# Decode attention with an MLP: the loop turn becomes one whole pair, and the last two V tiles come in key halves

## The chip, the cores and the metric

The kernel runs on one core of a Trainium2 chip. The metric is the device time of one execution in microseconds (us), from the first to the last instruction of the core with what lies around it; lower is better. The kernel before takes 1295.81 us, the median of three runs between 1295.5 and 1296.08.

## The reference, cut to what matters

```python
def reference(A_x, A_k_cache, A_v_cache, A_wq, A_wo, B_x, B_w1, B_b1, B_w2, B_b2):
    # B 8, one query position, D 640, 32 heads, 4096 keys, head size 128, F 1728, all bfloat16
    xn = _layernorm(A_x, axis=-1)
    q = heads(xn @ wq)                                        # [8, 32, 1, 128]
    scores = einsum("bhqd,bhkd->bhqk", q, k_cache) * 128 ** -0.5
    o = einsum("bhqk,bhkd->bhqd", softmax(scores), v_cache)
    attention = merge(o) @ wo
    h = gelu(layernorm(xn) @ w1 + b1)
    return A_x + attention + (h @ w2 + b2)
```

Each batch element and head has 4096 keys and as many values of 128 numbers. The K cache and the V cache together are 537 MB, and each number is used once.

## The kernel before, in words

**Tiles.** The work is cut into `NG` = 32 groups `g` of one batch element and eight heads. A group has a K tile and a V tile of 8 MB each. A tile is laid out as 128 partitions, 16 for each of the eight heads, by `NJ` = 256 keys by 128 numbers. K comes in two halves of 128 keys (`NKEY`), each 4 MB with a buffer of its own, so half `i` = 2g+s (s is 0 or 1) goes to `K_sb[:, s]`. V has one buffer, `V_sb`, of 8 MB for the whole tile. The code calls one group with both its K halves a pair.

**Scores of a K half.** The 128 keys are shared out. For the first 64 (`JD`), DVE multiplies K with the query, which is spread over the partitions in `qbc_sb`, adds the two halves of the products and reduces them, in three steps (`dve_chunk`). For the other 64 (`JP`), PE transposes K in eight blocks of eight keys (`pe_T`), ACT copies each block out of PSUM (`act_T`), and PE multiplies it with the queries of all eight heads (`pe_QK`). `dve_S` then selects the right head out of the eight in PSUM by a mask, and reduces; it is the select that the change moves.

**Select and PV of a group.** `dve_max` forms the maximum per head, `act_E` the exponentials `E_sb` and their row sums, and `dve_ex` spreads each weight over eight columns, all zero but that of its own head (`P_sb`, 128 x 2048). `pe_RS` adds the row sums over partitions, `dve_rinv` takes the reciprocal. `pe_PV` multiplies each of the 256 V blocks with its eight columns of P into one PSUM bank. `act_O` copies the result out, and `o_norm` scales it and stores it under a mask in `oM_sb`, on POOL for all groups but the last, on DVE for that one. Before the end `pe_ox` and `cp_ox` bring `oM_sb` into the form `oX_sb` that the product with wo needs (the first seven batch elements ahead, the eighth after the last group), `fin_wo` multiplies with wo in four pieces of 16, 10, 4 and 2 rows, and `fin_b` to `fin_d` transpose and store the output.

**Order.** All of it is written as a list of steps with a position (`at(pos, fn, ...)`, L634 to L713). Half `i` has the positions from 100 i on; sorted by position, the list gives the order of instructions on each engine. An engine runs its instructions strictly in that order and stops at a wait. All large loads are issued by SP, one after the other, into one DMA queue: in each group K half 2g+2, K half 2g+3, then V tile g+1. K half `i` waits until PE and DVE are through with half i-2 of the same buffer (`kt`, `km`), and V tile g waits until PV of group g-1 is done (`pv`). The V tile of group 30 comes in two halves, the second issued when the first has landed; that of group 31 comes whole. PV waits for the whole tile in all cases. wo's pieces are issued last.

**Prologue.** Ahead of group 0 stand the loads of wq, w1, w2 and K halves 0 and 1, the layer norms, the queries and the MLP. w1 lies in the buffer of K half 1, and w2 in that of V. So K half 1 waits for the MLP's first product and V tile 0 for its second (`mlp`) and for `pv` of the group before.

**Loop.** PE, DVE and ACT run `LOOPN` = 32 turns of a loop whose body is one group's steps; SP and POOL have straight code. `LOOP0` = -0.1 puts the border of a turn at position 200 g - 10: a turn is the select and PV of group g-1 and then the scores of group g. The first turn therefore has a select and a PV of a made-up group -1, on zeros that POOL writes to `Sd_sb` and to the part of `V_sb` that w2 does not fill (`vz`, `vz2`). The last select and PV stand behind the loop. In the sources `_replay_loop` and `looped` make the turns alike; a wait's value grows by the same step in each turn.

Of the kernel before, what the change touches and what calls it, by code (L numbers as in the profile page):

```python
# [13 lines left out]
P = 128  # L14
# [132 lines left out]
def bass_parallel_sum__gqa_block_cached__mixer_channel_mlp__decode_kernel(  # L147
# [22 lines left out]
    NQ = 2 * NG  # L170
    DC = D // P
# [5 lines left out]
    LOOP0, LOOPN = -0.1, NG  # L177
# [15 lines left out]
    with ExitStack() as es:  # L193
# [26 lines left out]
        oN_sb = sb("oN_sb", [P, HS], F32)  # L220
        head_i = sb("head_i", [P, HS], I32)
# [7 lines left out]
        oX_sb = sb("oX_sb", [P, NR, B], BF)  # L229
# [39 lines left out]
        ld_v, ld_vh = _Dma(sem("ld_v")), _Dma(sem("ld_vh"))  # L269
        ld_x, ld_b1, ld_b2, ld_wq, ld_w1, ld_w2b, st_a = (  # L270
            _Dma(sem(n)) for n in ("ld_x", "ld_b1", "ld_b2", "ld_wq", "ld_w1", "ld_w2b", "st_a"))
# [24 lines left out]
        def load_v(g, half=None):  # L296
            if half != 1:
                sp.wait(tk[("pv", g - 1)], tk["mlp"])
            else:
                sp.wait(tk[("vh", g)])  # L300
            lo, hi = (0, NJ) if half is None else (half * NKEY, (half + 1) * NKEY)
            d = ld_vh if half == 0 else ld_v
            tk[("vh" if half == 0 else "v", g)] = d.sig(sp.dma_start(
                V_sb[:, lo:hi, :], cache_src(A_v_cache, g, lo, hi)))

        def load_mlp():
            tk["w1"] = ld_w1.sig(sp.dma_start(w1_sb, B_w1.rearrange("(p c) f -> p c f", c=DC)))
            tk[("v", -1)] = tk["w2a"] = ld_v.sig(sp.dma_start(
                w2_sb[:, 0:FB, :], B_w2[0:FB * P, :].rearrange("(p c) n -> p c n", c=FB)))
            sp.wait(tk["vz"])  # L310
# [8 lines left out]
        def consts_pool():  # L319
            tk["iota"] = pool.sig(pool.iota(iota_i[:, :], [[1, P]], base=0, channel_multiplier=-1))  # L320
            tk["vz"] = pool.sig(pool.memset(M_sb[:, FB * D:(FB + 1) * D], 0.0))
            pool.memset(Sd_sb[:, :], 0.0)
# [162 lines left out]
        def dve_max(g):  # L485
            dve.wait(tk.get(("s", 2 * g + 1)), tk.get(("yr", (2 * g + 2) * NCH - 1)), tk["consts"])
# [17 lines left out]
        def dve_ex(g):  # L504
            dve.wait(tk[("E", g)], tk.get(("pv", g - 1)), tk.get(("rs", g - 1)), tk["mask8"])
            tk[("r8", g)] = dve.sig(dve.tensor_scalar(rs8_sb[:, :], mask8f[:, :], rs1_sb[:, 0:1], None, ALU.mult))
            tk[("ex", g)] = dve.sig(dve.tensor_tensor(
                P_sb[:, :, :], E_sb[:, :][:, :, None].to_broadcast([P, NJ, HS]),
                mask8b[:, :][:, None, :].to_broadcast([P, NJ, HS]), ALU.mult))
# [24 lines left out]
        def o_norm(g):  # L534
# [8 lines left out]
            if e is dve:  # L543
                PVB[0].used(dve, t)
# [267 lines left out]
```

## Time and profile before

| what | value |
|---|---|
| median of three runs | 1295.81 us |
| the profiled execution's own time | 1295.58 us |
| its span, first to last instruction | 1293.8 us |
| busy: PE, DVE, ACT, POOL | 779.9, 977.3, 581.4, 97.6 us |
| read from HBM | 551.80 MB, 427 GB/s over the span |
| V issued in the loop, issue to landing | 29.4 us, median |

The span lies 1.8 us below the execution's own time; that rest is around the instructions. In the lines of the profile below, PE is a matmul, PEld its weight load, SPq the issue of a DMA on SP's queue. A row of the timeline has the start in us, the length in us, the engine, the line, the operation, what it writes and reads with the shape, and how often; in brackets stands how long the engine was idle before it, and what ended that. Every row has line 104 because one helper records all instructions, so rows are told apart by their tiles. A row of DMA issues ends with the time from issue to landing.

### The profile page before, as it was taken

What the parts mean: (1) busy time and instruction counts of PE and PEld (TensorE: products, weight loads), DVE (VectorE), ACT (ScalarE), POOL (GpSimd) and SP (SyncE); (2) the same over time, 40 slices, a digit from 0 to 9 for tenths busy, and PEclk for the clock granted to TensorE, in tenths of its full rate; (3) what the DMA queues carried; (4) which work ended last, traced back from release to release, by engine and by line L of the source; (5) the groups of instructions that cost most, each with busy time, mean ns of one, the idle gap of its engine ahead of it and who ended that gap; (6) DMA issues with size and microseconds to landing.
All of it is one profiled execution on the core that took longest, in us unless ns stands there. A gap on an engine that the chain in (4) does not pass through costs nothing.

```text
span 1293.8 us, 38899 instructions
## 1 busy us (share of the span) xinstructions
PE 779.9 (60%) x17243; PEld 684.2 (53%) x17243; DVE 977.3 (76%) x1000; ACT 581.4 (45%) x682; POOL 97.6 (8%) x111
## 2 busy tenths in 40 slices
PE   4766655765555765654675555775555675555655
PEld 4655544654444665544564544665555565444544
DVE  4678779777779777779777779777779777779755
ACT  1544445553345553445553345554345553435532
POOL 3001000000000000000000000000000000000000
PEclk9956677776676675577766677666666775677766
DMA  9999999999999999999999999999999999999996
GB/s 395 423 421 430 431 435 432 444 426 440 418 437 433 441 426 448 412 435 434 440 428 444 419 431 435 438 428 446 420 429 436 436 436 438 422 433 431 435 428 261
DMA packets 15140, 552.01 MB, mean 427 GB/s; under 512 B 1740, under 2 KB 1813, under 8 KB 2070
## 3 DMA queue, kind: packets, MB, share of 16 engines
q1 hardware_dynamic: 15106, 551.80, 99.0%
q8 instruction: 10, 0.16, 0.1%
q14 instruction: 4, 0.03, 0.0%
q10 hardware_dynamic: 20, 0.02, 0.0%
HBM read 551.80 MB, written 0.01 MB: 427 GB/s over the span
## 4 chain that ended last, share of the span: by engine, by line
DMA 63%; PE 14%; DVE 9%; ACT 8%; issue 6%; DVEq 0%; ACTq 0%; POOL 0%; SPq 0%
DMA K_sb<-in_A_k_cache_dram 58%; ACT KT_sb L104 7%; DVE Y_sb L104 7%; PE TR_ps L104 6%; PE PV_ps L104 4%; DMA V_sb<-in_A_v_cache_dram 3%; PE S_ps L104 3%; DMA W_sb<-in_A_wq_dram 1%; DVE P_sb L104 1%; PE CH_ps L104 1%; DVE SM_sb L104 1%; DVE Sd_sb L104 0%; PE ACC_ps L104 0%; DVE mx_sb L104 0%; ACT E_sb L104 0%
## 5 line engine op out<-in xcount | busy, mean ns | idle before, releaser
L104 ACT ACTIVATE KT_sb<-TR_ps 128x1024 bf16<-128x1024 bf16 x512 | 501.4, 1022 | 100.4 <-PE TR_ps L104 97.8
L104 DVE TENSOR_TENSOR Y_sb<-K_sb,qbc_sb 128x2688 bf16<-128x2688 bf16 (+1 forms) x192 | 300.6, 1566 | 217.5 <-DMA K_sb<-in_A_k_cache_dram 217.5
L104 PE MATMUL TR_ps<-ident_bf,K_sb 128*128 128x128 bf16 x4096 | 383.9, 255 | 11.0 <-DMA K_sb<-in_A_k_cache_dram 9.8
L104 PEld LDWEIGHTS TR_ps<-ident_bf,K_sb 128*128 128x128 bf16 x4096 | 301.1, 115 | 14.3 <-DMA K_sb<-in_A_k_cache_dram 12.1
L104 DVE TENSOR_REDUCE Sd_sb<-Y_sb 128x21 f32<-128x1344 bf16 (+1 forms) x192 | 302.5, 1576 | 6.6
L104 PE MATMUL PV_ps<-P_sb,V_sb 128*128 128x8 bf16 x8448 | 230.9, 168 | 63.9 <-DVE P_sb L104 51.3
L104 PEld LDWEIGHTS PV_ps<-P_sb,V_sb 128*128 128x128 bf16 x8448 | 228.0, 104 | 67.0 <-issue 56.2
L104 PE MATMUL S_ps<-qrep_sb,KT_sb 128*128 128x8 bf16 x4096 | 193.8, 177 | 110.6 <-ACT KT_sb L104 98.2
L104 PEld LDWEIGHTS S_ps<-qrep_sb,KT_sb 128*128 128x128 bf16 x4096 | 147.3, 100 | 190.4 <-ACT KT_sb L104 187.2
L104 PE MATMUL CH_ps<-rs_sb,ones_f 128*128 128x8 f32 x66 | 19.5, 369 | 289.0 <-DVE rs_sb L104 288.8
L104 DVE TENSOR_TENSOR Y_sb<-Y_sb 128x1344 bf16<-128x1344 bf16 (+1 forms) x192 | 167.5, 873 | 6.6
L104 PEld LDWEIGHTS CH_ps<-rs_sb,ones_f 128*128 128x128 f32 x66 | 16.5, 311 | 293.6 <-ACT E_sb L104 285.9
L104 ACT ACTIVATE oU_sb<-PV_ps 128x8 f32<-128x8 f32 x32 | 5.7, 177 | 318.2 <-PE PV_ps L104 318.2
L104 POOL TENSOR_TENSOR oN_sb<-oU_sb,ri_sb 128x8 f32<-128x8 f32 x32 | 45.4, 1419 | 860.5 <-DVE ri_sb L104 806.4
L104 DVE TENSOR_TENSOR P_sb<-E_sb,mask8b 128x2048 bf16<-128x2048 bf16 x33 | 75.4, 2284 | 0.0
L104 ACT ACTIVATE qbc_sb<-CH_ps 128x128 bf16<-128x128 f32 x33 | 9.1, 277 | 134.4 <-DVE Y_sb L104 129.2
L104 ACT ACTIVATE E_sb<-Sd_sb,NB_sb 128x256 bf16<-128x256 f32 x33 | 16.7, 507 | 117.3 <-DVE NB_sb L104 117.3
L104 DVE TENSOR_TENSOR SM_sb<-S_ps,mask8f 128x512 f32<-128x512 f32 x64 | 43.6, 681 | 22.5 <-PE S_ps L104 22.5
L104 ACT ACT_TABLE_LOAD x34 | 43.6, 1283 | 8.5 <-DVE qT_sb L104 4.2
L104 DVE TENSOR_REDUCE Sd_sb<-SM_sb 128x64 f32<-128x512 f32 x64 | 43.9, 687 | 2.2
L104 POOL COPY qrep_sb<-qT_sb 128x128 bf16<-128x128 bf16 x33 | 12.8, 388 | 306.3 <-PE S_ps L104 300.9
L104 DVE TENSOR_SCALAR rs_sb<-mask8f,rs_sb 128x8 f32<-128x8 f32 x33 | 7.6, 231 | 30.0 <-ACT E_sb L104 30.0
(71 smaller groups left out, 162.7 us busy)
## 6 DMA issues: line engine op xcount, KB each, us to landing
K_sb<-in_A_k_cache_dram SPq DMA_DIRECT2D x64, 4096.0 KB, 25.5
V_sb<-in_A_v_cache_dram SPq DMA_DIRECT2D x2, 4096.0 KB, 19.5
W_sb<-in_A_wq_dram SPq DMA_DIRECT2D x1, 5120.0 KB, 15.4
W_sb<-in_A_wo_dram SPq DMA_DIRECT2D x1, 2560.0 KB, 28.0
K_sb<-in_B_w_dram SPq DMA_DIRECT2D x1, 2160.0 KB, 20.0
V_sb<-in_B_w_dram SPq DMA_DIRECT2D x1, 2080.0 KB, 25.6
W_sb<-in_A_wo_dram SPq DMA_DIRECT2D x1, 1600.0 KB, 31.3
W_sb<-in_A_wo_dram SPq DMA_DIRECT2D x1, 640.0 KB, 32.4
```

Source lines behind the costliest of these rows:

```text
L104: inst = getattr(e, name)(*a, **k)
```

## The change

- **Turn.** `LOOP0` is 0.057, so that the border of a turn is at position 200 g + 5.7: a turn is the scores of group g, its select and its PV. The made-up group, its zeros and the waits on them go; the steps run over `range(NG)`. `act_O` now also runs for group 31. V tile 0 waits for the MLP alone.
- **V.** The tiles of groups 30 and 31 (`g >= G2`) come in two key halves, each half's landing counted by a semaphore of its own (`ld_v[0]`, `ld_v[1]`), with no wait for the landing of the other. The second half of tile 30 stands in SP's queue behind K half 62, that of tile 31 directly behind its first half. PV waits for the first half ahead of matmul 0 and for the second ahead of matmul 128. For groups below 30 the whole tile counts on `ld_v[0]`; a memset of POOL at the start raises `ld_v[1]` by 16 x 30, so that the second wait has passed for these.
- **P.** `dve_ex` makes P in two products of 128 keys, and PV waits for each half.
- **Select.** `dve_S` of a group's first half goes from position 86 to 160: behind the first two of the second half's three steps on DVE.
- **Reciprocal and end.** `dve_rinv` goes from position 45 to 4.2, right behind PE's row sums. For the last group `o_norm` first multiplies reciprocal and mask, beside PV, and then needs one product from PSUM in place of two. The first seven `oX` products and their copy go behind the last PV, and `oX_sb` is stored with the batch element outside.

```diff
@@ -168,13 +168,14 @@
     NQ = 2 * NG
+    G2 = NG - 2
     DC = D // P
...
     CHMAX = 22
-    LOOP0, LOOPN = -0.1, NG
+    LOOP0, LOOPN = 0.057, NG
     PAD = 96
@@ -218,6 +219,7 @@
         oN_sb = sb("oN_sb", [P, HS], F32)
+        riM_sb = sb("riM_sb", [P, HS, DQ], F32)
         head_i = sb("head_i", [P, HS], I32)
@@ -226,7 +228,7 @@
         oU_sb = sb("oU_sb", [P, HS], F32)
-        oX_sb = sb("oX_sb", [P, NR, B], BF)
+        oX_sb = sb("oX_sb", [P, B, NR], BF)
         x_sb = sb("x_sb", [B, D], BF)
@@ -266,9 +268,9 @@
         ld_k = [_Dma(sem(f"ld_k{s}")) for s in range(2)]
-        ld_v, ld_vh = _Dma(sem("ld_v")), _Dma(sem("ld_vh"))
-        ld_x, ld_b1, ld_b2, ld_wq, ld_w1, ld_w2b, st_a = (
-            _Dma(sem(n)) for n in ("ld_x", "ld_b1", "ld_b2", "ld_wq", "ld_w1", "ld_w2b", "st_a"))
+        ld_v = [_Dma(sem(f"ld_v{u}")) for u in range(2)]
+        ld_x, ld_b1, ld_b2, ld_wq, ld_w1, ld_w2a, ld_w2b, st_a = (
+            _Dma(sem(n)) for n in ("ld_x", "ld_b1", "ld_b2", "ld_wq", "ld_w1", "ld_w2a", "ld_w2b", "st_a"))
         ld_wo = [_Dma(sem(f"ld_wo{q}")) for q in range(len(WO_CUT) - 1)]
@@ -294,20 +296,15 @@
         def load_v(g, half=None):
-            if half != 1:
-                sp.wait(tk[("pv", g - 1)], tk["mlp"])
-            else:
-                sp.wait(tk[("vh", g)])
+            sp.wait(tk.get(("pv", g - 1)), tk["mlp"])
             lo, hi = (0, NJ) if half is None else (half * NKEY, (half + 1) * NKEY)
-            d = ld_vh if half == 0 else ld_v
-            tk[("vh" if half == 0 else "v", g)] = d.sig(sp.dma_start(
-                V_sb[:, lo:hi, :], cache_src(A_v_cache, g, lo, hi)))
+            u = half or 0
+            tk[("v", g, u)] = ld_v[u].sig(sp.dma_start(V_sb[:, lo:hi, :], cache_src(A_v_cache, g, lo, hi)))
 
...
             tk["w1"] = ld_w1.sig(sp.dma_start(w1_sb, B_w1.rearrange("(p c) f -> p c f", c=DC)))
-            tk[("v", -1)] = tk["w2a"] = ld_v.sig(sp.dma_start(
+            tk["w2a"] = ld_w2a.sig(sp.dma_start(
                 w2_sb[:, 0:FB, :], B_w2[0:FB * P, :].rearrange("(p c) n -> p c n", c=FB)))
-            sp.wait(tk["vz"])
             tk["w2b"] = ld_w2b.sig(sp.dma_start(w2_sb[0:FLAST, FB, :], B_w2[FB * P:F, :]))
@@ -318,16 +315,16 @@
             tk["iota"] = pool.sig(pool.iota(iota_i[:, :], [[1, P]], base=0, channel_multiplier=-1))
-            tk["vz"] = pool.sig(pool.memset(M_sb[:, FB * D:(FB + 1) * D], 0.0))
-            pool.memset(Sd_sb[:, :], 0.0)
             tk["heads"] = pool.sig(pool.iota(head_i[:, :], [[HP, HS]], base=0, channel_multiplier=-1))
...
             pool.memset(mx_sb[:, :], 0.0)
-            pool.memset(ones_f[:, :], 1.0)
+            pool.memset(ones_f[:, :], 1.0).call[3] = (ld_v[1].sem, 16 * G2)
+            ld_v[1].n = 16 * G2
+            for g in range(G2):
+                tk[("v", g, 1)] = (ld_v[1].sem, 16 * (g + 1))
             t = pool.sig(pool.memset(nsc_sb[:, :], -SCALE), PAD)
             tk["consts"] = t
-            tk["vz2"] = pool.sig(pool.memset(M_sb[:, (FB + 1) * D:NJ * DH].bitcast(F32), 0.0))
 
@@ -483,7 +480,7 @@
         def dve_max(g):
-            dve.wait(tk.get(("s", 2 * g + 1)), tk.get(("yr", (2 * g + 2) * NCH - 1)), tk["consts"])
+            dve.wait(tk[("s", 2 * g + 1)], tk[("yr", (2 * g + 2) * NCH - 1)], tk["consts"])
             t = dve.sig(dve.tensor_reduce(mx_sb[:, 0:1], Sd_sb[:, :], AX.X, ALU.max))
@@ -504,9 +501,11 @@
             tk[("r8", g)] = dve.sig(dve.tensor_scalar(rs8_sb[:, :], mask8f[:, :], rs1_sb[:, 0:1], None, ALU.mult))
-            tk[("ex", g)] = dve.sig(dve.tensor_tensor(
-                P_sb[:, :, :], E_sb[:, :][:, :, None].to_broadcast([P, NJ, HS]),
-                mask8b[:, :][:, None, :].to_broadcast([P, NJ, HS]), ALU.mult))
+            for u in range(2):
+                r = slice(u * NKEY, (u + 1) * NKEY)
+                tk[("ex", g, u)] = tk[("ex", g)] = dve.sig(dve.tensor_tensor(
+                    P_sb[:, r, :], E_sb[:, r][:, :, None].to_broadcast([P, NKEY, HS]),
+                    mask8b[:, :][:, None, :].to_broadcast([P, NKEY, HS]), ALU.mult))
 
@@ -521,8 +520,9 @@
             PVB[0].use(pe)
-            pe.wait(tk[("ex", g)], tk[("v", g)], tk["vz2"])
             for j in range(NJ):
+                if j % NKEY == 0:
+                    pe.wait(tk[("ex", g, j // NKEY)], tk[("v", g, j // NKEY)])
                 last = pe.matmul(PV_ps[:, 0, 0:HS], V_sb[:, j, :], P_sb[:, j, :], start=(j == 0), stop=(j == NJ - 1))
@@ -532,20 +532,24 @@
         def o_norm(g):
-            hp, b = divmod(max(g, 0), B)
+            hp, b = divmod(g, B)
             dst = oM_sb[:, b, hp * HS:(hp + 1) * HS, :]
-            e, src = (pool, oU_sb[:, :]) if g < NG - 1 else (dve, PV_ps[:, 0, 0:HS])
-            if e is dve:
+            if g < NG - 1:
+                pool.wait(tk["mask"], tk[("oU", g)], tk[("ri", g)])
+                t = pool.sig(pool.tensor_tensor(oN_sb[:, :], oU_sb[:, :], ri8_sb[:, :], ALU.mult))
+                pool.wait(t)
+                tk[("on", g)] = pool.sig(pool.tensor_tensor(
+                    dst, oN_sb[:, :][:, :, None].to_broadcast([P, HS, DQ]),
+                    mask_sb[:, :][:, None, :].to_broadcast([P, HS, DQ]), ALU.mult))
+            else:
+                dve.wait(tk["mask"], tk[("ri", g)])
+                t = dve.sig(dve.tensor_tensor(
+                    riM_sb[:, :, :], ri8_sb[:, :][:, :, None].to_broadcast([P, HS, DQ]),
+                    mask_sb[:, :][:, None, :].to_broadcast([P, HS, DQ]), ALU.mult))
                 PVB[0].use(dve)
-                dve.wait(tk.get(("on", g - 1)))
-            e.wait(tk["mask"], tk.get(("oU", g)), tk[("ri", g)])
-            t = e.sig(e.tensor_tensor(oN_sb[:, :], src, ri8_sb[:, :], ALU.mult))
-            if e is dve:
-                PVB[0].used(dve, t)
-            e.wait(t)
-            tk[("on", g)] = e.sig(e.tensor_tensor(
-                dst, oN_sb[:, :][:, :, None].to_broadcast([P, HS, DQ]),
-                mask_sb[:, :][:, None, :].to_broadcast([P, HS, DQ]), ALU.mult))
+                dve.wait(t, tk[("on", g - 1)])
+                tk[("on", g)] = PVB[0].used(dve, dve.sig(dve.tensor_tensor(
+                    dst, PV_ps[:, 0, 0:HS][:, :, None].to_broadcast([P, HS, DQ]), riM_sb[:, :, :], ALU.mult)))
 
@@ -558,7 +562,7 @@
             PVB[1].use(e)
-            o, i_ = oX_sb[:, :, b0:b1].rearrange("p c b -> p b c"), OX_ps[:, b0:b1, :]
+            o, i_ = oX_sb[:, b0:b1, :], OX_ps[:, b0:b1, :]
             tk[("oX", b1)] = PVB[1].used(e, e.sig(
@@ -568,7 +572,7 @@
                     last = pe.matmul(ACC_ps[:, k * B:(k + 1) * B], wo_sb[:, c, k * P:(k + 1) * P],
-                                     oX_sb[:, c, :], start=False, stop=(c == NR - 1), skip_group_check=True)
+                                     oX_sb[:, :, c], start=False, stop=(c == NR - 1), skip_group_check=True)
             if hi == NR:
@@ -659,25 +663,24 @@
         at(-738, pe_mlp2)
-        for g in range(-1, NG):
+        for g in range(NG):
             o = (2 * g + 2) * Q
...
             at(o + 4, pe_RS, g)
+            at(o + 4.2, dve_rinv, g)
             at(o + 5, pe_PV, g)
-            if g < NG - 1:
-                at(o + 5.5, act_O, g)
-            at(o + 45, dve_rinv, g)
-            at(o + 46, o_norm, g)
+            at(o + 5.5, act_O, g)
+            at(o + (46 if g < NG - 1 else 6), o_norm, g)
         for i in range(NQ):
...
             if s == 0:
-                at(o + 5.6, load_v, g, *((0,) if g == NG - 2 else ()))
-            elif g == NG - 2:
+                at(o + 5.6, load_v, g, *((0,) if g >= G2 else ()))
+            if g >= G2 and s == NG - 1 - g:
                 at(o + 6, load_v, g, 1)
@@ -686,7 +689,7 @@
                 at(o + 10 + 75.0 * c / NCH, dve_chunk, i, c)
-            at(o + 86, dve_S, i)
+            at(o + (160 if s == 0 else 86), dve_S, i)
             if s == 1:
@@ -700,8 +703,8 @@
         o = NQ * Q
-        at(o + 1, pe_ox, 0, B - 1)
-        at(o + 2.5, cp_ox, 0, B - 1)
+        at(o + 7, pe_ox, 0, B - 1)
+        at(o + 7.5, cp_ox, 0, B - 1)
         for q in range(len(WO_CUT) - 1):
```

## The prediction

> **What bounds the kernel now.** I read the page from the top: busy shares, queues, chain of waits; then busy time by stretches of one pair; then each load's issue and landing; then the order of time at both ends.
>
> ```profile
> span 1293.8 us, 38899 instructions
> q1 hardware_dynamic: 15106, 551.80, 99.0%
> DMA 63%; PE 14%; DVE 9%; ACT 8%; issue 6%; DVEq 0%; ACTq 0%; POOL 0%; SPq 0%
> ```
>
> SP's queue fills the sixteen DMA engines for 99.0% of the span, and no compute engine owns much of the chain. All 552 MB must move, so time can come only from stretches in which this queue is empty, and from what follows its last byte.
>
> ```profile
> 45.49:84.27 38.78, 24.68 (x529) 21.65 (x528) 27.66 (x28) 18.67 (x23) 2.26 (x3) 0.78 0.98 418
> 239.39:278.17 38.78, 23.10 (x526) 20.18 (x522) 29.97 (x31) 18.34 (x22) 2.97 (x3) 0.71 1.00 433
> 1208.89:1247.67 38.78, 16.84 (x408) 14.61 (x405) 36.13 (x36) 13.90 (x16) 3.02 (x3) 0.68 1.00 432
> ```
>
> These are three stretches of one pair's length (busy PE, PEld, DVE, ACT, POOL, clock, DMA share, GB/s). In the middle and near the end DMA is full at 432 to 433 GB/s, DVE, the busiest engine, at 30.0 of 38.78 us. So whatever shortens a middle pair's engine work gains nothing. Only the first stretch lacks bytes: (433-418)/433 x 38.78 = 1.3 us. The two ends are what is left.
>
> **Part 1, the front: no made-up pair.** SP's issues and the landing times (last column of the second fence):
>
> ```profile
> 30.63 0.33 SPq L104 DMA_DIRECT2D K_sb<-in_A_k_cache_dram  x1
> 45.49 0.33 SPq L104 DMA_DIRECT2D V_sb<-in_A_v_cache_dram  x1
> ```
> ```profile
> K_sb<-in_A_k_cache_dram SPq DMA_DIRECT2D x1, 4096.0 KB, 16.3
> V_sb<-in_A_v_cache_dram SPq DMA_DIRECT2D x1, 23.3
> V_sb<-in_A_v_cache_dram SPq DMA_DIRECT2D x1, 22.0
> ```
>
> K(1) lands at 30.63+16.3 = 46.9, V(0) at 45.49+23.3 = 68.8: 21.9 apart. The last V tile, issued (below) while the queue is full, lands 19.3 behind its forerunner. So the queue ran dry for **2.5 us**. V(0) is that late because `load_v` waits for the made-up pair's PV:
>
> ```profile
> 31.85 1.27 PE L104 MATMUL ACC_ps<-hT_sb,V_sb 128*128 128x8 bf16 x39
> 35.45 3.79 PE L104 MATMUL PV_ps<-P_sb,V_sb 128*128 128x8 bf16 x136 [1.60 <-DVE P_sb L104]
> 42.09 3.37 PE L104 MATMUL PV_ps<-P_sb,V_sb 128*128 128x8 bf16 x120 [2.86 <-issue]
> 37.26 1.56 DVE L104 TENSOR_TENSOR Y_sb<-K_sb,qbc_sb 128x2688 bf16<-128x2688 bf16 x1 [1.94 <-DMA K_sb<-in_A_k_cache_dram]
> 16.20 1.23 PE L104 MATMUL CH_ps<-xT_sb,W_sb 128*128 128x8 bf16 x40 [3.12 <-DMA W_sb<-in_A_wq_dram]
> ```
>
> The MLP's last matmul ends at 33.1 (31.85+1.27); then come 256 matmuls on zeros, with a 2.86 us hole, up to 45.46. Without them V(0) waits for the MLP alone and is issued at about 33.2, 13.7 us before K(1) lands. Taken: the gap of 2.5 us closes. Bounds: 0 and 2.5. The next loads aren't late in its place: K(0) is there at 37.26, when PE now multiplies zeros until 45.46; PE then starts some 8 us earlier, and K(2), K(3) and V(1) are issued about as much earlier.
>
> The dropped memsets and `vz` waits I cost at 0: PE's first real work waits for wq at 16.20, whatever DVE and POOL do before. The dropped select instructions on DVE, ACT and POOL lie beside the MLP.
>
> **Part 2, the middle: 0.** Per pair the P product becomes two, `dve_rinv` stands before the next products, the first half's select moves behind two products of the second, PV waits in the middle. All lie under a queue that is full. The spare at V's issue, the next to run dry:
>
> ```profile
> V_sb<-in_A_v_cache_dram SPq DMA_DIRECT2D x31, 29.4
> ```
> ```profile
> 1242.18 0.20 DVE L104 RECIPROCAL ri_sb<-CH_ps 128x8 f32<-128x8 f32 x1
> ```
>
> A V tile takes 19.3 of the queue's own time and lands 29.4 after issue, so 10 us are queued ahead. Start-up, by the front, needs up to 46.9-45.49+2.5 = 3.9 of them; **6 us per pair** are cover. Two P products cost +0.15 us by the fit of part 3. The reciprocal (0.20) now waits for PE's row-sum product, with the next pair's products queued behind it on DVE; that product is started ahead of P and is over before P is. PV's new wait holds its own second half and the next pair's transposes on PE; for thirty of the 32 pairs the V semaphore in it is set at the start, and P's second half is 1.2 us of DVE, while the first 128 matmuls take 3.5. The later select holds only its score bank, which PE writes again one pair later. SP's order K, K, V is unchanged; nothing is moved past its queue but the half tiles of the end, issued once the PV before is done instead of after their first half landed.
>
> **Part 3, the end.** Issues, landings, and engine work in order of time:
>
> ```profile
> 1222.50 0.33 SPq L104 DMA_DIRECT2D V_sb<-in_A_v_cache_dram  x1
> 1226.06 0.33 SPq L104 DMA_DIRECT2D K_sb<-in_A_k_cache_dram  x1
> 1248.97 0.33 SPq L104 DMA_DIRECT2D V_sb<-in_A_v_cache_dram  x1
> ```
> ```profile
> V_sb<-in_A_v_cache_dram SPq DMA_DIRECT2D x1, 4096.0 KB, 19.4
> K_sb<-in_A_k_cache_dram SPq DMA_DIRECT2D x1, 4096.0 KB, 25.6
> W_sb<-in_A_wo_dram SPq DMA_DIRECT2D x1, 2560.0 KB, 28.0
> W_sb<-in_A_wo_dram SPq DMA_DIRECT2D x1, 1600.0 KB, 31.3
> W_sb<-in_A_wo_dram SPq DMA_DIRECT2D x1, 320.0 KB, 32.6
> ```
> ```profile
> L104 SPq DMA_DIRECT2D W_sb<-in_A_wo_dram x4: 425/477/537, 1249.4 to 1250.9; - x4
> 1241.95 6.99 PE L104 MATMUL PV_ps<-P_sb,V_sb 128*128 128x8 bf16 x256 [9.05 <-DMA V_sb<-in_A_v_cache_dram]
> 1258.47 0.69 DVE L104 TENSOR_TENSOR SM_sb<-S_ps,mask8f 128x512 f32<-128x512 f32 x1 [12.03 <-PE S_ps L104]
> 1259.80 1.55 DVE L104 TENSOR_TENSOR Y_sb<-K_sb,qbc_sb 128x2688 bf16<-128x2688 bf16 x1
> 23.52 0.46 PE L104 MATMUL CH_ps<-xT_sb,K_sb 128*128 128x8 bf16 x5
> 1266.77 0.37 PE L104 MATMUL S_ps<-qrep_sb,KT_sb 128*128 128x8 bf16 x8 [0.54 <-ACT KT_sb L104]
> 1271.81 0.68 DVE L104 TENSOR_TENSOR SM_sb<-S_ps,mask8f 128x512 f32<-128x512 f32 x1
> 1226.10 0.28 ACT L104 ACTIVATE qbc_sb<-CH_ps 128x128 bf16<-128x128 f32 x1 [4.24 <-DVE Y_sb L104]
> 1275.14 1.14 ACT L104 ACTIVATE oX_sb<-PV_ps 128x224 bf16<-128x224 f32 x1
> 1275.41 2.28 DVE L104 TENSOR_TENSOR P_sb<-E_sb,mask8b 128x2048 bf16<-128x2048 bf16 x1
> 1277.75 6.64 PE L104 MATMUL PV_ps<-P_sb,V_sb 128*128 128x8 bf16 x243 [1.60 <-DVE P_sb L104]
> 1285.08 0.51 PE L104 MATMUL PV_ps<-P_sb,V_sb 128*128 128x8 bf16 x13 [0.68 <-issue]
> 1286.68 4.55 PE L104 MATMUL ACC_ps<-oX_sb,W_sb 128*128 128x8 bf16 x160 [0.39 <-DVE oX_sb L104]
> 1291.26 0.20 DVE L104 CAST resT_sb<-ACC_ps 128x40 bf16<-128x40 f32 x1 [4.64 <-PE ACC_ps L104]
> ```
>
> Landings: V(30)'s second half 1241.9, K(63) 1251.7, V(31) 1271.0, the pieces of wo 1277.4, 1281.2 and, issued at 1250.9, 1283.5. Today PE stands 9.05 us for V(30)'s second half, runs all 256 matmuls, then K(62)'s scores; DVE stands 12.03 us for these before it may touch K(63), which landed at 1251.7. From there to the end there is only compute, past wo's landing.
>
> After the change, first with the landings of before:
> - PV(30)'s first half runs early. The second starts at 1241.9 and takes 128 x 6.99/256 = 3.5: done **1245.4** (now 1248.9).
> - K(62)'s scores are done 1258.47-1248.94 = 9.5 later, 1254.9. K(63)'s took 1266.77+0.37-1258.47 = 8.7 more: 1263.6.
> - DVE begins K(63) at its landing, 1251.7. One product-add-reduce step takes (1271.81-1259.80)/3 = 4.0. Two steps: 1259.7; K(62)'s select (1259.80-1258.47 = 1.33): 1261.0; third step 1265.0; both score waits have passed. From select to P took 1275.41-1271.81 = 3.6: **1268.6** (now 1275.4).
> - Half a P product, linear between the 512- and 2048-column rows (0.69, 2.28), is 1.22: 1269.8 and 1271.0. V(31)'s halves land at 1261.4 and 1271.0. PV ends 1269.8+7.0 = **1276.8** (now 1285.6).
> - From there to the first wo matmul took 1286.68-1285.59 = 1.09. Added: the seven other `oX` products and their ACT copy now come behind PV, and the last product's bank waits for that copy. At its old 1.14 us the copy makes it 2.2; at the pace of ACT's copy of 128 contiguous columns (0.28) it would be 1.4 to 1.6. Bounds 0.9 to 2.2; taken 1.4, because DVE in turn does one small product less there and the output is now contiguous: 1278.2.
> - 160 matmuls take 4.55 us; alone they would end at 1282.8. But the last piece of wo lands at 1283.5, and its ten need 0.5: **1284.0**. The bound is again DMA, with some 1.2 us to spare. The `oX` columns, now strided, I cost at 0: the score products, too, read every sixteenth column of theirs, and eight take 0.37 (the 1266.77 row), the pace of PV's contiguous ones. Upper bound: the MLP's strided weights take 0.46 for five against 1.23 for wq's forty, 0.06 more each over 128 columns, so 0.004 over eight: 0.6 in 160.
> - From there to the end: 1293.8-1291.26 = 2.54. End 1286.5: **7.3 earlier**. The moved end of the loop turn, now between PV and the next transposes, is bounded by 0 and the 2.86 of the front hole; I take 0.
>
> A price against the split: the Trainium skill, DMA: Bandwidth & Descriptors, section Anatomy of one DMA, gives every transfer a fixed cost of about 2.0 us; here there is one transfer more, so by it the sum would be 2 us worse. The trace differs where the queue is full: K(63)'s 4 MB landed 9.8 behind their forerunner, V(31)'s 8 MB 19.3, so two smaller transfers cost 0.2 more.
>
> **Sum.** Landings move by the 2.5 of part 1 right through the full middle, the end by 7.3: 9.8 us. The profiled execution took 1295.58, so **1285.8**; its time lies 0.23 below the median shown, inside the noise of about 0.2% (2.6 us) that a measurement can tell from no change.
>
> **Rivals.**
> - *PE must fetch code at the new turn end.* For: the 2.86 us hole in the first turn, 0.68 in the last PV. Against: neither hole recurs in the middle. Ahead of K(62)'s transposes it would cost 2.9-1.4 = 1.5 at P; after the loop it would delay the first wo matmul by 2.9, of which the spare absorbs 1.2: **1287.5** (1289.0 with both). Chance 0.13. The Trainium skill, Runtime: NRT & Kernel Launch, Instruction fetch mechanics, says that a taken branch out of the fetched window forces such a fetch; the trace of before can't show it, since PE waits for DVE at its turn end.
> - *The front gap stays*, because the queue, not PV, held V(0). Against: V(0) lands 2.5 later than a queued tile would. Only the end's 7.3: **1288.3**. Chance 0.07.
> - *The change doesn't do what it says*: thirty V tiles stay whole and only P is halved; if the two last don't overlap either, because both halves land together, PE blocks K(62) until 1248.9, 3.5 later; K(63)'s scores have 1.4 to spare (1263.6 against 1265.0) and wo 1.2, so 0.9 is lost: **1286.7**. Chance 0.05.
> - *Slower: refetch in each turn.* If PE's loop body no longer stayed loaded, every turn would stop between PV and the transposes that free K. Up to the 6 us of cover it costs nothing; above, each us costs one per turn, 31, so from 6.3 us on the gain is eaten. At 7 us the kernel would be at 1285.8+31 = **1317**. The first pass's hole was 2.86, below the deciding point. Chance 0.04.
>
> **How the numbers follow.** Forecast within 1 us 0.66; the rivals 0.13, 0.07, 0.05, 0.04; 0.05 for a gain that comes out within 0.2% of none. The range reaches from 1284.3 (the whole tail at its lower bounds, wo some tenths earlier) to 1289.0 (the faster rivals): about 0.87. Faster by over 0.2%: 0.66+0.13+0.07+0.05 = 0.91; within 0.05; slower 0.04.
>
> **What would show it.** V(0) issued near 33 and landing 19.3 behind K(1). Middle stretches still 433 GB/s. No 12 us DVE wait for scores at the end; K(63)'s first product at its landing. PV(31) done 2 to 7 us before the last piece of wo lands, and the last ten matmuls waiting for DMA. Wrong, if an "issue" hole opens on PE behind PV, if GB/s falls in the middle, or if PV(31) ends later than wo's last landing.

## The result, and the profile after

| | before | after |
|---|---|---|
| median, us (6 runs each, taken in turn) | 1295.94 | 1286.28 |
| lowest and highest, us | 1295.03 to 1296.37 | 1285.7 to 1286.89 |
| ratio, 95% interval | | 0.9926 [0.9913, 0.9939] |
| profiled execution, us | 1295.58 | 1285.81 |
| its span, us | 1293.8 | 1284.0 |

The span is 9.8 us shorter. From the page of the kernel after: SP's queue, and the chain of waits by engine.

```profile
q1 hardware_dynamic: 15250, 551.80, 99.7%
DMA 70%; PE 9%; ACT 7%; DVE 7%; issue 6%; SPq 0%; ACTq 0%; DVEq 0%
```

The same 551.80 MB take 99.7% of a shorter span (99.0% before); DMA's share of the chain grows from 63% to 70%, at the cost of PE, DVE and ACT.

**Front.** The timeline of the kernel after, at the made-up group's old place, and the landing times of K half 1 and V tile 0:

```profile
30.76 0.33 SPq L104 DMA_DIRECT2D K_sb<-in_A_k_cache_dram  x1
33.28 0.33 SPq L104 DMA_DIRECT2D V_sb<-in_A_v_cache_dram  x1
37.25 1.89 PE L104 MATMUL TR_ps<-ident_bf,K_sb 128*128 128x128 bf16 x16 [4.00 <-DMA K_sb<-in_A_k_cache_dram]
73.81 3.67 PE L104 MATMUL PV_ps<-P_sb,V_sb 128*128 128x8 bf16 x127 [2.88 <-issue]
```
```profile
K_sb<-in_A_k_cache_dram SPq DMA_DIRECT2D x1, 4096.0 KB, 16.1
V_sb<-in_A_v_cache_dram SPq DMA_DIRECT2D x1, 33.0
```

V(0) is issued at 33.28, not at 45.49. K(1) lands at 30.76+16.1 = 46.9, V(0) at 33.28+33.0 = 66.3: 19.4 apart (21.9 before), which is the queue's own time for a V tile. PE takes K(0) as soon as it has landed. The 2.9 us hole in PE's first real PV is still there; it only lies under a full queue now. Stretches, the first row of the kernel before, the others of the kernel after (columns as in the prediction):

```profile
30.00:46.00 16.00, 11.00 (x342) 10.61 (x343) 11.03 (x10) 2.37 (x6) 0.17 (x1) 1.00 0.93 395
30.00:46.00 16.00, 10.68 (x199) 9.20 (x197) 8.63 (x7) 8.78 (x11) 0.00 (x0) 1.00 1.06 453
239.39:278.17 38.78, 24.89 (x527) 21.95 (x523) 30.08 (x32) 18.89 (x22) 0.73 (x3) 0.65 1.00 433
1199.10:1237.88 38.78, 20.24 (x387) 17.31 (x387) 35.81 (x36) 18.06 (x21) 0.73 (x3) 0.68 1.01 433
```

The stretch at the made-up group's old place moved 395 GB/s before and moves 453 now. The middle and the stretch ahead of the end run at 433 GB/s, as before.

**End.** The order of time in the kernel after, and the landing times of wo's pieces, which are issued from 1244.0 to 1245.5:

```profile
1230.85 3.58 PE L104 MATMUL PV_ps<-P_sb,V_sb 128*128 128x8 bf16 x128 [0.46 <-DVE P_sb L104]
1239.61 3.55 PE L104 MATMUL PV_ps<-P_sb,V_sb 128*128 128x8 bf16 x128 [5.19 <-DMA V_sb<-in_A_v_cache_dram]
1243.49 1.28 ACT L104 ACT_TABLE_LOAD   x1
1244.78 1.94 ACT L104 ACTIVATE KT_sb<-TR_ps 128x1024 bf16<-128x1024 bf16 x2
1249.21 1.56 DVE L104 TENSOR_TENSOR Y_sb<-K_sb,qbc_sb 128x2688 bf16<-128x2688 bf16 x1 [5.20 <-DMA K_sb<-in_A_k_cache_dram]
1257.11 0.68 DVE L104 TENSOR_TENSOR SM_sb<-S_ps,mask8f 128x512 f32<-128x512 f32 x1
1263.87 0.69 DVE L104 TENSOR_TENSOR SM_sb<-S_ps,mask8f 128x512 f32<-128x512 f32 x1 [1.25 <-PE S_ps L104]
1267.48 2.35 DVE L104 TENSOR_TENSOR P_sb<-E_sb,mask8b 128x1024 bf16<-128x1024 bf16 x2
1268.76 6.99 PE L104 MATMUL PV_ps<-P_sb,V_sb 128*128 128x8 bf16 x256 [0.46 <-DVE P_sb L104]
1276.00 0.36 ACT L104 ACTIVATE oX_sb<-PV_ps 128x224 bf16<-128x224 f32 x1
1276.97 4.48 PE L104 MATMUL ACC_ps<-oX_sb,W_sb 128*128 128x8 bf16 x160 [0.29 <-DVE oX_sb L104]
1281.49 0.20 DVE L104 CAST resT_sb<-ACC_ps 128x40 bf16<-128x40 f32 x1 [4.58 <-PE ACC_ps L104]
```
```profile
W_sb<-in_A_wo_dram SPq DMA_DIRECT2D x1, 2560.0 KB, 30.7
W_sb<-in_A_wo_dram SPq DMA_DIRECT2D x1, 320.0 KB, 35.4
```

PV(30) runs in halves and ends at 1243.16. The 12.03 us in which DVE waited for K(62)'s scores are gone: DVE takes K(63) when it lands (1249.21), and K(62)'s select at 1257.11 waits for nothing. P comes at 1267.48 instead of 1275.41, and the hole of 0.68 in the last PV has gone. wo's last piece lands at 1245.5+35.4 = 1280.9, and the 160 products of wo run unbroken up to 1281.45. Two things are new: an ACT table load between PV(30) and K(62)'s first copy, and a wait of DVE of 1.25 us for K(63)'s scores.

### The profile page after: what moved, and what is told of

Same layout as the page of the kernel before. It is cut to its first block, busy times and chain, and to the rows that moved or that the text cites. A ratio compares the mean times of both kernels' runs of the same rounds, so it can differ in the third digit from the quotient of the medians.

```text
span 1284.0 us, 38493 instructions
## 1 busy us (share of the span) xinstructions
PE 786.3 (61%) x16985; PEld 691.4 (54%) x16985; DVE 969.3 (75%) x1024; ACT 581.3 (45%) x680; POOL 25.6 (2%) x106
## 3 DMA queue, kind: packets, MB, share of 16 engines
q1 hardware_dynamic: 15250, 551.80, 99.7%
HBM read 551.80 MB, written 0.01 MB: 430 GB/s over the span
## 4 chain that ended last, share of the span: by engine, by line
DMA 70%; PE 9%; ACT 7%; DVE 7%; issue 6%; SPq 0%; ACTq 0%; DVEq 0%
DMA K_sb<-in_A_k_cache_dram 68%; ACT KT_sb L104 7%; DVE Y_sb L104 6%; PE TR_ps L104 5%; DMA V_sb<-in_A_v_cache_dram 2%; PE S_ps L104 2%; PE PV_ps L104 1%; PE ACC_ps L104 0%; DVE Sd_sb L104 0%; SPq L104 0%; DVE P_sb L104 0%; DVE SM_sb L104 0%; ACT L104 0%; DVE mx_sb L104 0%; ACTq L102 0%
## 5 line engine op out<-in xcount | busy, mean ns | idle before, releaser
L104 PE MATMUL TR_ps<-ident_bf,K_sb 128*128 128x128 bf16 x4096 | 399.7, 262 | 51.0 <-DMA K_sb<-in_A_k_cache_dram 50.6
L104 PEld LDWEIGHTS TR_ps<-ident_bf,K_sb 128*128 128x128 bf16 x4096 | 314.1, 118 | 54.3 <-DMA K_sb<-in_A_k_cache_dram 53.2
L104 PE MATMUL PV_ps<-P_sb,V_sb 128*128 128x8 bf16 x8192 | 224.2, 168 | 25.3 <-DVE P_sb L104 14.8
L104 PEld LDWEIGHTS PV_ps<-P_sb,V_sb 128*128 128x128 bf16 x8192 | 221.3, 104 | 28.5 <-DVE P_sb L104 17.8
L104 DVE TENSOR_TENSOR P_sb<-E_sb,mask8b 128x1024 bf16<-128x1024 bf16 x64 | 75.3, 1218 | 0.0
L104 POOL COPY qrep_sb<-qT_sb 128x128 bf16<-128x128 bf16 x33 | 9.6, 290 | 677.2 <-PE S_ps L104 660.9
L104 POOL TENSOR_TENSOR oN_sb<-oU_sb,ri_sb 128x8 f32<-128x8 f32 x31 | 7.1, 229 | 558.4 <-ACT oU_sb L104 558.4
```

The costliest lines, as they stand in the source:

```text
L104: inst = getattr(e, name)(*a, **k)
```

## The experiments

**Theory**: 2.5 us come from V(0)'s issue, 7.3 from three edits at the end (select 3.4, V halves up to 3.4, P halves 1.1), and the end now lies on the edge between compute and wo's landing. **Rivals**: the new order of the turn gives the tail's gain by itself; wo's landing holds the end, so that compute there is free; PE refetches code in every turn, and cover hides it. All kernels but three (e5b, e8, e11) are the kernel after with one edit. Medians stand beside 1295.5 to 1295.9 for the kernel before on the same chip. The last two columns compare with the kernel after: its median of 1286.28, and the span of its profiled execution. A span, like every row shown, is that of one execution; the times of a kernel's executions spread by 0.1 us (e6) to 2.1 us (e10), in e11 by 5.1, so the two columns can differ by more than a microsecond.

| run | median, us | ratio to before, 95% | span, us | median against after | span against after |
|---|---|---|---|---|---|
| e1_v0_late | 1288.18 | 0.994 [0.9924, 0.9957] | 1286.9 | +1.90 | +2.9 |
| e2_v_whole | 1286.53 | 0.993 [0.9913, 0.9946] | 1284.7 | +0.25 | +0.7 |
| e2b_pv_both | 1289.2 | 0.9952 [0.9935, 0.9968] | 1286.5 | +2.92 | +2.5 |
| e3_select_early | 1289.56 | 0.9953 [0.9936, 0.9969] | 1287.5 | +3.28 | +3.5 |
| e4_p_whole | 1286.81 | 0.9932 [0.9915, 0.9949] | 1284.6 | +0.53 | +0.6 |
| e5b_tail_undone | 1294.12 | 0.9989 [0.9979, 0.9998] | 1292.0 | +7.84 | +8.0 |
| e6_act_turn | 1285.75 | 0.9924 [0.9908, 0.9941] | 1284.0 | -0.53 | 0.0 |
| e7_wo_less | 1286.08 | 0.9926 [0.9909, 0.9942] | 1284.2 | -0.20 | +0.2 |
| e8_act_turn_wo_less | 1284.72 | 0.9916 [0.9899, 0.9932] | 1283.4 | -1.56 | -0.6 |
| e9_pe_extra | 1291.11 | 0.9961 [0.9947, 0.9975] | 1290.1 | +4.83 | +6.1 |
| e10_two_straight | 1289.58 | 0.9951 [0.9934, 0.9969] | 1288.5 | +3.30 | +4.5 |
| e11_two_straight_warm | 1293.35 | 0.9982 [0.9972, 0.9991] | 1292.5 | +7.07 | +8.5 |

**V(0) issued where it was before (e1).**

```diff
-                at(o + 5.6, load_v, g, *((0,) if g >= G2 else ()))
+                at(o + (60 if g == 0 else 5.6), load_v, g, *((0,) if g >= G2 else ()))
-            sp.wait(tk.get(("pv", g - 1)), tk["mlp"])
+            sp.wait(tk.get(("pv", g - 1)), tk["mlp"], tk[("qk", 5)] if g == 0 else None)
```

> The changed kernel, but V tile 0 is issued only after PE's sixth score block of K half 0 (near 45.2 us, where it was issued before the change) instead of right after the MLP. If the front gain is V's issue time: V(0) lands some 22 us after K(1) instead of 19.4, every later landing moves by 2.5 us, span 1284.0 + 2.5 = 1286.5, time near 1288.8. If the gain came from the work that the made-up pair no longer does on the engines: no more than 0.3 us.

Its V(0), issue and time to landing:

```profile
44.98 0.33 SPq L104 DMA_DIRECT2D V_sb<-in_A_v_cache_dram  x1
```
```profile
V_sb<-in_A_v_cache_dram SPq DMA_DIRECT2D x1, 24.3
```

It lands at 69.3, 3.0 later than in the kernel after, and the span is 2.9 longer, the median 1.9; 2.5 was expected. The work of the made-up group is absent here too, so the front's gain is V's issue time.

**Whole V tiles (e2).**

```diff
-    G2 = NG - 2
+    G2 = NG
```

> The changed kernel with V tiles 30 and 31 loaded whole, one landing each. PE then starts all 256 matmuls of PV(30) when the tile has landed (1239.5) and frees itself 3.5 us later than now. If the end is one chain without spare (PV(30), scores of K 62, scores of K 63, P, PV, wo), as the trace after suggests (DVE waits 1.25 us for the scores of K 63): span +3.4, 1287.4. If the spare of the prediction were there (1.4 us at the scores, 1.2 at wo): +0.9, 1284.9. If the halves don't matter: 0.

This run doesn't isolate the halves. A whole V(30) stands in the queue ahead of K(62), so it is there when P is, PV runs at 1230.76 without a stop, and K(62) lands 9.6 us later instead (1239.3 against 1229.7). It undoes the halves and their order in the queue at once, so its +0.7 is no price of the halves.

**PV waits for both halves, the loads as they are (e2b).**

```diff
-                    pe.wait(tk[("ex", g, j // NKEY)], tk[("v", g, j // NKEY)])
+                    pe.wait(tk[("ex", g, j // NKEY)], tk[("v", g, 0)], tk[("v", g, 1)])
```

> The changed kernel with all loads as they are (order, halves, semaphores), but PV waits for both halves of V ahead of its first matmul. PV(30) then starts at 1239.6 with all 256 matmuls and frees PE 3.5 us later. If the end is one chain without spare (scores of K 62, scores of K 63, P, PV, wo): span +3.4, 1287.4. If the spare of the prediction were there (1.4 at the scores, 1.2 at wo): +0.9, 1284.9. If the order of the loads was what the halves bought, and not the early first half of PV: 0.

The order of time at its end:

```profile
1239.62 6.97 PE L104 MATMUL PV_ps<-P_sb,V_sb 128*128 128x8 bf16 x256 [9.21 <-DMA V_sb<-in_A_v_cache_dram]
1257.66 0.69 DVE L104 TENSOR_TENSOR SM_sb<-S_ps,mask8f 128x512 f32<-128x512 f32 x1 [0.46 <-PE S_ps L104]
1266.36 0.69 DVE L104 TENSOR_TENSOR SM_sb<-S_ps,mask8f 128x512 f32<-128x512 f32 x1 [3.18 <-PE S_ps L104]
```

The 9 us wait of before is back, PV(30) ends 3.43 later (1246.59 against 1243.16), and both selects wait for scores. Only 2.5 reach the end, because K(63)'s scores take 8.7 us here, from 1257.62 to 1266.32, and 10.0 in the kernel after, from 1253.84 to 1263.84. So the halves are worth 3.4 where they act, and 2.5 with what the scores then gave back (2.9 by the medians).

**The first half's select at its old place (e3).**

```diff
-            at(o + (160 if s == 0 else 86), dve_S, i)
+            at(o + 86, dve_S, i)
```

> The changed kernel with the first half's select back at its old place, ahead of all products of the second half. DVE then waits for the scores of K 62 (1253.8) before it touches K 63 (there since 1249.2): 1.3 us of select and 12.1 us of three steps put the last select at 1267.3 instead of 1263.9. Chain without spare: span +3.4, 1287.4. With 1.2 us of spare before wo's last landing: +2. In the middle of the kernel: nothing, 433 GB/s.

```profile
1254.09 0.69 DVE L104 TENSOR_TENSOR SM_sb<-S_ps,mask8f 128x512 f32<-128x512 f32 x1 [9.87 <-PE S_ps L104]
1267.42 0.68 DVE L104 TENSOR_TENSOR SM_sb<-S_ps,mask8f 128x512 f32<-128x512 f32 x1
```

In these rows DVE stands 9.87 us for K(62)'s scores, the last 4.7 of them with K(63) landed (1249.4); the second select follows three product steps later, 3.55 behind that of the kernel after. As expected.

**P in one product (e4).**

```diff
-            for u in range(2):
-                r = slice(u * NKEY, (u + 1) * NKEY)
...
+            tk[("ex", g, 0)] = tk[("ex", g, 1)] = tk[("ex", g)] = dve.sig(dve.tensor_tensor(
+                P_sb[:, :, :], E_sb[:, :][:, :, None].to_broadcast([P, NJ, HS]),
...
```

> The changed kernel with P in one product again. The last PV starts one half product later (2.28 against 1.22 us). Chain without spare: span +1.1, 1285.1. With the predicted spare of 1.2 us before wo's last landing: 0. Per pair in the middle nothing in both cases; if the half product gained in every pair, 32 x 1.1 = 35 us would be lost.

```profile
1269.37 6.99 PE L104 MATMUL PV_ps<-P_sb,V_sb 128*128 128x8 bf16 x256 [1.53 <-DVE P_sb L104]
```

PV starts 2.34 behind P instead of 1.28. That is 1.06 at its place, of which some 0.45 came back, since K(63)'s scores took 9.4 us in this run. The medians (1286.81 and 1286.28) lie inside each other's spread, so the 0.6 rests on the traces of two single executions.

**The three edits of the tail undone together (e5b)** (the last three diffs in one kernel; V(0) stays early).

> The changed kernel with PV waiting for both halves, the first half's select at its old place and P in one product: turn, loads and front stay as changed, the end computes as before. Scores of K 62 3.5 us later (1257.3), select 1.3, three steps 12.1: last select at 1270.7 instead of 1263.9, and PV 1.1 later: +7.9, span 1291.9. That is before's 1293.8 less the front's 2.5, plus what the end has lost otherwise. If the three edits hide the same thing, less than that.

```profile
1257.50 0.69 DVE L104 TENSOR_TENSOR SM_sb<-S_ps,mask8f 128x512 f32<-128x512 f32 x1 [13.35 <-PE S_ps L104]
1276.77 6.99 PE L104 MATMUL PV_ps<-P_sb,V_sb 128*128 128x8 bf16 x256 [1.52 <-DVE P_sb L104]
```

All but 1.8 of the 9.8 us are gone (1.4 by the medians), so the new turn does not give the tail's gain. The three prices at their places, 3.5+3.43+1.06, make the 8.0. That it is more than the 7.3 of the change: K(62)'s scores are done at 1257.5, 1.5 later than before's 1258.47 less the front's 2.5; the last PV has no hole, which gives 0.85 back (6.99 against 7.84 from its first to its last matmul).

**ACT's turn border moved by itself (e6)**, back to where the table load has idle time.

```diff
...
         for m in range(LOOPN + 1):
             at((LOOP0 + 2 * m) * Q, mark)
+        for m in range(LOOPN):
+            at((1.9 + 2 * m) * Q, mark_act)
...
```

> The changed kernel with ACT's turn border alone put back ahead of the select (31 turns; the first scores and the last select stand outside the loop). The activation table load of 1.28 us that opens each of ACT's turns then lies where ACT waits for the maximum, and not ahead of the first score block after PV. Scores of K 62 and 63 end 1.3 us earlier, the wait of DVE (1.25 us) goes. But wo's last piece lands at 1280.9 and its ten products need 0.5, so the end can move by 0.1 to 0.2 us only: span 1283.9. If nothing of DMA stood behind it: -1.25, 1282.75.

```profile
1244.09 1.94 ACT L104 ACTIVATE KT_sb<-TR_ps 128x1024 bf16<-128x1024 bf16 x2 [0.72 <-PE TR_ps L104]
1263.55 0.69 DVE L104 TENSOR_TENSOR SM_sb<-S_ps,mask8f 128x512 f32<-128x512 f32 x1 [0.93 <-PE S_ps L104]
1276.64 4.76 PE L104 MATMUL ACC_ps<-oX_sb,W_sb 128*128 128x8 bf16 x160 [0.28 <-DVE oX_sb L104]
1280.96 0.35 PEld L104 LDWEIGHTS ACC_ps<-oX_sb,W_sb 128*128 128x128 bf16 x10 [0.15 <-DMA W_sb<-in_A_wo_dram]
```

The first copy starts 0.69 earlier, K(63)'s scores are done 0.32 earlier, and the wo products are begun 0.33 earlier; but the last ten now wait for wo, and the end stays. It is the lowest median of all versions that compute everything, but within the spread of the kernel after. Its four executions lie within 0.09 us, those of the kernel after within 1.19: that fits an end held by the last landing here and by compute there, but no run was made to show it.

**wo's landing taken away.** e7 and e8 load one row of each of wo's four pieces and leave the other rows out, so they multiply with what lies in the buffer; e8 has e6's edit too.

```diff
-                wo_sb[:, lo:hi, :], A_wo.rearrange("(p c) n -> p c n", c=NR)[:, lo:hi, :]))
+                wo_sb[:, lo:lo + 1, :], A_wo.rearrange("(p c) n -> p c n", c=NR)[:, lo:lo + 1, :]))
```

> The changed kernel with only one row out of each of wo's four pieces loaded (the rest of the product with wo runs on what lies in the buffer: that part of the load is left out). DMA then ends some 11 us earlier. If compute holds the end, as the unbroken 160 matmuls from 1276.97 suggest: 0 to -0.1, span 1284.0. If wo's last landing holds it, as predicted: up to -1.2.

> ACT's turn border ahead of the select, and one row out of each of wo's four pieces loaded (the rest of the product with wo runs on what lies in the buffer: that part of the load is left out). With neither the table load nor wo's landing in the way the end moves by the whole 1.25 us: span 1282.7. If the table load were not what made the scores late: 1284.0.

K(62)'s scores, from the end of PV(30), in e8 and in the kernel after (columns as above), and DVE's last select in e8:

```profile
1243.23:1253.23 10.00, 8.60 (x131) 7.37 (x129) 4.72 (x4) 8.04 (x9) 0.45 (x2) 0.67 0.99 426
1243.16:1253.84 10.68, 8.56 (x130) 7.34 (x129) 5.41 (x5) 9.32 (x10) 0.45 (x2) 0.66 1.02 439
```
```profile
1263.29 0.69 DVE L104 TENSOR_TENSOR SM_sb<-S_ps,mask8f 128x512 f32<-128x512 f32 x1 [0.57 <-PE S_ps L104]
```

Without wo's bytes the kernel after is hardly faster (+0.2 by the span, -0.20 by the median): compute alone holds its end. With the table load out of the way too, the profiled execution is 0.6 shorter. At the same clock, 0.67 against 0.66, the load's 0.68 reaches the end of K(62)'s scores whole; in e6 only 0.3 of it did, where these scores ran at 0.60 and took 10.40. The other 0.57 of DVE's wait is still there, so half of the expected 1.25 had another cause than the table load. The profiled execution is the slowest of e8's four; their median lies 1.56 below that of the kernel after. Either obstacle taken away alone gives at most 0.5, because the two lie within 0.3 us of each other.

**More work for PE in each turn (e9)**: 128 matmuls on zeros behind each PV.

```diff
             tk[("pv", g)] = PVB[0].used(pe, pe.sig(last))
+            for j in range(128):
+                pe.matmul(PV_ps[:, 1, 256:256 + HS], zeros_sb[:, :], zeros_sb[:, 0:HS], start=True, stop=True)
```

> The changed kernel with 128 more matmuls on zeros (3.5 us, into a bank that nobody reads then) behind each PV, that is at the new turn end. If the full DMA queue covers the middle: it costs only at the end, 3.5 us ahead of the scores of K 62 and 3.5 behind the last PV, +7, span 1291. If a stop at the turn end were paid per turn (the slower rival): 31 x 3.5 = +108.

A turn in the middle, and the added work at the end:

```profile
239.39:278.17 38.78, 27.57 (x650) 24.73 (x648) 30.09 (x32) 18.49 (x23) 1.64 (x3) 0.66 1.00 433
```
```profile
1243.02 3.56 PE L104 MATMUL PV_ps<-zeros_sb 128*128 128x8 bf16 x128
```

32 x 3.56 = 114 us of work cost 6.1 (4.8 by the medians), and the middle keeps 433 GB/s: the price is that of the two last turns, less the 0.7 that the scores gave back (20.0 against 20.7 for K(62) and K(63)). A turn has at least 3.6 us of cover, which fits the 6 us estimated. At a turn border in the middle, the kernel after (first row) and e9:

```profile
463.84 1.89 PE L104 MATMUL TR_ps<-ident_bf,K_sb 128*128 128x128 bf16 x16 [1.60 <-DMA K_sb<-in_A_k_cache_dram]
```
```profile
462.07 3.55 PE L104 MATMUL PV_ps<-zeros_sb 128*128 128x8 bf16 x128
465.50 1.88 PE L104 MATMUL TR_ps<-ident_bf,K_sb 128*128 128x128 bf16 x16
```

In the kernel after PE waits 1.60 us for K there, and a short stop for code could hide in that wait. In e9 the wait is gone, and PE goes from the last product on zeros to the transposes without idle time. Its waits over the whole span show no stop at a border but 0.3 us once, in the first turn. So PE does not refetch in each turn.

**The last two groups written out behind the loop (e10)**, to have no turn border near the end; in e11 also 176 matmuls in PE's wait for V(30)'s second half, to keep the clock up.

```diff
-    LOOP0, LOOPN = 0.057, NG
+    LOOP0, LOOPN = 0.057, NG - 2
```
```diff
             for j in range(NJ):
+                if g == G2 and j == NKEY:
+                    for w in range(176):
+                        pe.matmul(PV_ps[:, 1, 256:256 + HS], V_sb[:, w % NKEY, :], P_sb[:, w % NKEY, :],
+                                  start=True, stop=True)
```

> The changed kernel with 30 loop turns on PE, DVE and ACT and the last two groups written out behind the loop. No turn border, and so no activation table load, lies between PV(30) and the scores of K 62. If the table load makes the scores late, they start 0.7 us earlier, as with ACT's border moved; their end depends on PE's granted clock. Span 1284.0, between 1283.8 (wo's last landing) and 1284.7 (if PE must fetch the written-out code and stops for it as long as once in the last PV of before, 0.68).

> The same with two groups written out, and 176 more matmuls (4.8 us, into a bank that nobody reads then) in PE's wait for V(30)'s second half, 1234.4 to 1239.6. If the scores of K 62 and K 63 took 10.7 and 10.0 us after the change instead of the 9.5 and 8.7 taken over from before because PE came out of that wait at half the clock (granted 0.50 from 1243 to 1248, 0.65 to 0.67 over both), the clock there is now near 1.0, the scores of K 63 end by 1262 instead of 1263.8, and DVE does not wait for them. The end moves by no more than 0.2 below 1284.0, because wo lands last. If the clock is not the cause: scores as in the run without the extra matmuls.

Both expectations miss. PE's order of time in e10, and its instruction queue on the page:

```profile
1236.46 0.40 PE L104 MATMUL PV_ps<-P_sb,V_sb 128*128 128x8 bf16 x9 [2.33 <-issue]
1246.94 0.41 PE L104 MATMUL PV_ps<-P_sb,V_sb 128*128 128x8 bf16 x10 [2.58 <-issue]
1279.52 0.54 PE L104 MATMUL PV_ps<-P_sb,V_sb 128*128 128x8 bf16 x15 [1.57 <-issue]
```
```profile
q8 instruction: 16, 0.26, 0.1%
```

PE stops in code that it runs for the first time. The first hole lies in its wait for V(30)'s second half; the second is on the path, as are 1.47 us by which that half came later (1241.08 against 1239.61), and the third stands in the last PV; the scores of K(62) and K(63) gave 1.6 back (19.1 against 20.7). Twice as many instruction packets (8 in the kernel after) came through the DMA engines. The trace has the time of each: in the three holes above PE goes on 1.3 to 1.5 us after the end of one such packet. e11's own holes, 2.06, 2.90 and 3.17 around PV(30), buried what it was to test: what sets the clock in K(62)'s and K(63)'s scores stays open. Its ten executions lie between 1291.03 and 1296.17.

**The scores' time and the granted clock.** K(63)'s scores, from the end of K(62)'s, in the kernels before, after, e4 and e2b (length, busy PE, PEld, DVE, ACT, POOL, clock, DMA share, GB/s):

```profile
1258.43:1267.14 8.71, 6.63 (x129) 5.23 (x126) 8.49 (x8) 7.76 (x8) 0.00 (x0) 1.00 0.83 361
```
```profile
1253.84:1263.84 10.00, 8.66 (x129) 7.34 (x126) 8.61 (x8) 7.91 (x8) 0.00 (x0) 0.67 0.98 423
```
```profile
1253.94:1263.37 9.43, 7.69 (x129) 6.37 (x126) 8.55 (x8) 7.76 (x8) 0.00 (x0) 0.82 1.03 441
```
```profile
1257.62:1266.32 8.70, 6.63 (x128) 5.22 (x126) 5.42 (x5) 7.76 (x8) 0.00 (x0) 1.00 1.00 429
```

The same instructions take 8.7 us at clock 1.00, 9.4 at 0.82 and 10.0 at 0.67; of the engines' busy times only PE's follows. e10 and e11 ran at 1.00 and 8.7, e2_v_whole at 1.00 and 8.8, e5b, e7 and e9 at 0.81 to 0.84 and 9.5, e1, e3, e6 and e8 at 0.66 to 0.67 and 10.0. K(62)'s scores took 9.5 in the kernel before at 0.84, with no table load ahead. The link is read across these fourteen kernels; no run forced the clock, so it is not shown to be the cause.

## Why the prediction was right, and which step was off

- **Front, 2.5: right.** V(0) was issued at 33.28 (33.2 forecast) and landed 19.4 behind K(1). That this moves the end is shown by e1: 3.0 later at the front, 2.9 in the span, 1.9 in the median.
- **Middle, 0: right.** 433 GB/s with 3.6 us more of PE work per turn, too (e9). The upper bound on the strided `oX` columns was not needed: 160 products take 4.48, before 4.55.
- **End, 7.3: the sum right, one term mis-sized.** Landings came 2.4 to 2.6 earlier than before, PV(30) ended at 1243.16 (forecast 1245.4-2.5). The term is the scores' time, "9.5 later" and "8.7 more", taken over from before: they took 10.68 and 10.0. 0.68 of the first is ACT's table load (e8): the prediction took the moved end of the turn at 0 and looked at PE's code alone there. The rest goes with a clock of 0.66 and 0.67 where before had 0.84 and 1.00. That ate the 1.4 of spare ahead of the last select, which waits 1.25, and P came at 1267.48 instead of 1266.1. Two smaller terms: from PV's end to the first wo product 1.22 (1.4 forecast; the copy takes 0.36 where its price was bounded by 1.14), and half a P product 1.218 (1.22). The reciprocal and end edits were not taken back by themselves; the three prices of the tail, 8.0 together, already exceed its 7.3.
- **"The bound is again DMA, with some 1.2 us to spare": wrong.** The spare was eaten by the late P, and the last ten products did not wait. Compute ended at 1281.45; the forecast for wo's last ten was 1284.0-2.5 = 1281.5. That the total came out exact is luck in part: compute was late by about as much as the 1.2 of spare. An end of compute up to 1.2 later than assumed ends at the same place, at wo's landing; with scores slower still, each us would have counted.
- **The split's price of 2 us, quoted in the prediction: did not come.** V(31)'s second half landed at 1268.6 (issued at 1243.6, 25.0 to landing), 19.4 behind K(63); the whole tile came 19.3 behind it before. The Trainium skill, DMA: Bandwidth & Descriptors, Anatomy of one DMA, fits that figure to transfers on GpSimd's path, while SP issues these.
- **The rival of code at the turn end: not in the looped code.** PE's waits over the whole span of the kernel after have two rows for it:

```profile
PE PV_ps L104 <- issue: 5.3, 2, 2.9
PE TR_ps L104 <- issue: 0.3, 1, 0.3
```

Two stops, both in the first turn's PV, 0.3 us at the first turn's border, and none behind PV at the end. The Trainium skill, Runtime: NRT & Kernel Launch, Instruction fetch mechanics, expects a stop at a taken branch that leaves the fetched window and calls the cost of sequential fetch mostly hidden. 31 jumps back cost PE no stop but that 0.3 (e9 shows it where PE has no other wait at the border); by the rule, a turn's code would lie within that window, which no run shows. On the second point the trace differs: code on its first pass does stop PE, 2.88 us in the first turn. The rival's price was thus of the right size; e10 paid it by leaving the loop.
- **Front gap stays, halves don't overlap, refetch in each turn**: none came. e1 and e2b show what the first two would have cost, +2.9 and +2.5 (+1.9 and +2.9 by the medians); the forecasts were +2.5 and +0.9. The second was too low for the same reason as above: the spare that was to absorb it did not exist.

## What to carry to other kernels

Where one DMA queue is full throughout, look for gains only where it runs dry and behind its last byte: 9.8 us came from there, and 114 us of added PE work, nearly all of it elsewhere, cost five to six. At a tail, add up both chains, the engines' and the last transfer's; when they end within a few tenths, neither removing compute nor removing bytes shows much alone. Carry a stage's duration over from another place only with its granted clock beside it; here one stage took 8.7 us at 1.00 and 10.0 at 0.67. When a loop's turn is moved, look at what each engine does at the border: here it was ACT, not PE, that did something.

## What the runs showed of the hardware

- **First passes.** PE's stops without a releaser in PV and in wo's products lie 127 or 128 matmuls apart (the first turn of the kernel after: 125, hole of 2.88, 127, hole of 2.44, 4). An instruction packet is 0.26 MB / 16 = 16 KB. The stops lasted 1.57 to 3.17 us at the end of e10 and e11 while the large queue was full, and 0.68 and 0.70 (the last PV of the kernel before, wo's products in e11) when it had just run out. In each of them PE goes on 1.2 to 1.6 us after the end of one instruction packet, in the first turns of these kernels and of e9 too; so the stops are put down to the fetch of code.
- **The table load follows ACT's turn border.** There are 34 loads of 1.28 us in both kernels with their 32 turns, 33 in e6 with 31 turns of ACT and 32 in e10 with 30. Before, they lay where ACT waits for the maximum (the row below is of the kernel before), after, at the new border between PV and the first copy.

```profile
1226.39 1.28 ACT L104 ACT_TABLE_LOAD   x1
```

- **The copy of 224 columns** takes 0.36 us into contiguous `oX_sb` and took 1.14 into a strided one; the copies stand at different places of the two kernels, and no run changed the stride alone.
